# Batch 1's k'q moved from bare steps to pairs beside expert blocks, with the first block one step earlier

## The chip, the core and the metric

The kernel runs on one core of one Trainium2 chip. The time is the device time of one execution in microseconds (us), as the median of several runs. TensorE (PE in the rows) multiplies matrices and has a weight load that runs beside it (PEld). VectorE is DVE, ScalarE is ACT, GpSimd is POOL. SyncE (SP) issues most of the DMAs. POOL issues the indirect ones, which write rows to computed addresses.

## What is computed

Four batches of attention over channels, and then a mixture of experts over all 20224 tokens. In short:

```python
# B, N, C = 4, 5056, 256; 8 experts of 256 -> 1024 -> 256
qn = q / norm(q, axis=1);  kn = k / norm(k, axis=1)
a  = softmax(kn.T @ qn / tau)             # 256 x 256 per batch
x  = v @ a                                # tokens x 256
e  = argmax(x @ w_gate + modality_bias[modality_id])
out[t] = softmax_prob[t, e] * relu(x[t] @ w1[e]) @ w2[e]
```

Everything is in float32. Each product is made of three products of rounded halves (high by high, high by low, low by high).

## The kernel before

A batch is cut into ten steps of 512 tokens (the last has 448), so there are 40 steps in all, numbered g = 0 to 39. The kernel has four kinds of work.

- **k'q** (`kq_pieces(b, s)`, lines 219 to 314) loads 512 rows of q and k, splits each into high and low halves (ACT line 257, DVE line 258), squares them for the norms (ACT line 272, added up by DVE line 274) and multiplies them into the batch's 256 by 256 matrix (PE lines 283 and 287). In the steps named in `SELF`, the norm comes from PE instead (line 294), and the square and the addition fall away. A whole batch of it must be done before that batch's softmax.
- **softmax** (`softmax_pieces`) turns the matrix into the weights of the batch.
- **v a** (`va_pieces(b, s)`) loads 512 rows of v, transposes them (PE line 460), multiplies them by the weights (PE line 476, 24 matmuls of 264 columns), routes each token to its expert (DVE lines 485 to 533, with three small matmuls `rp`, lines 512 to 514), and writes the rows to the expert's list `xs` in memory by four indirect DMAs (POOL line 407).
- **an expert block** (`block_pieces`) takes 512 rows of one expert from `xs` (SP line 596), loads that expert's weights in two halves (SP lines 615 and 619), splits them (lines 634 and 635), transposes the rows (`xtp`, PE line 645), and multiplies twice (`hp`, line 663, and `y`, line 683). There are 40 blocks.

Batch 0's k'q runs alone at the start. Then the loop at line 767 goes through the steps. In step g it interleaves the v a of step g, the k'q of the next batch for the same step number, and a block if one is due. After the step, `pick` (lines 553 to 582, on DVE) chooses an expert that has 512 rows waiting, and if none has, a spare block of padding. `slots_by(g)` says how many blocks are to be chosen after step g: the first after step 3. A block runs `LAG` = 4 steps after its choice, so the first in step 7. Its loads are issued one step ahead, and its first weight split and its transposes (`prep`) stand at the end of the step before it. Blocks that do not fall in the 40 steps run one after another behind them: seven of them.

The text's order is not yet the order of the queues. The framework lays out each engine's queue ahead of time with a planner: it takes the earliest instruction in the text whose inputs and buffer are there by the planner's own estimate of durations, and so pulls later work forward into a gap that it expects. On the chip each queue then runs in that order and waits where the estimate was short.

Buffers limit what can be pulled forward. The q and k tiles of batch 1 have two buffers each, and those of steps 2, 3 and 4 borrow the three buffers of the expert weights (`w1r`, `w2r`). The split halves have two buffers per half step, with the buffers of the blocks (`xh`, `xl`, `hh`, `hl`) lent to the early steps, as the conditions on `START` say.

Of the kernel before, what the change touches and what calls it, by code (L numbers as in the profile page):

```python
# [18 lines left out]

def _interleave(*streams):  # L20

    lists = [list(s) for s in streams if s]
    total = [len(x) for x in lists]
    at = [0] * len(lists)
    while any(a < n for a, n in zip(at, total)):
        i = min(
            (i for i in range(len(lists)) if at[i] < total[i]),
            key=lambda i: ((at[i] + 0.5) / total[i], i),
        )
        lists[i][at[i]]()  # L30
        at[i] += 1
# [3 lines left out]
def kernel(  # L35
# [20 lines left out]
    NS = -(-N // STEP)  # L56
# [14 lines left out]
    LAG = 4  # L71

    SELF = {
        "q": [{1, 4, 7}, set(), set(), set()],
        "k": [set(range(NS)), set(range(4)), set(), set()],
    }
    START = 3

    def parts(s):
        return P if s < NS - 1 else PL  # L80
# [137 lines left out]
    def kq_pieces(b, s):  # L218
        pp = parts(s)
        st = {}  # L220
        t0 = s * STEP

        def load():
            if s == 0:
                gram[b] = [
                    ps1.tile([P, 2 * C], F32, tag=f"{'y' if b == 0 else 'g'}{m}", name=f"g{m}_{b}")
                    for m in range(CH)
                ]
                acc[b] = p1.tile([P, 2, 2 * C], F32, tag="acc", name=f"acc_{b}", bufs=2)
                for n in ("k", "q"):  # L230
                    if SELF[n][b]:
                        selfp[n, b] = ps2.tile([P, CH, 2 * P], F32, tag="h", name=f"self{n}_{b}")
                        norm[n, b] = p1.tile([P, CH], F32, tag=f"n{n}", name=f"n{n}_{b}")
            for n, src, tag in (("q", q, "w1r"), ("k", k, "w2r")):
                if (b == 0 and s % 5 >= 2) or (b == 1 and 2 <= s < START + 2):
                    st[n] = p3.tile([P, TT, C], F32, tag=tag, name=f"{n}_{b}_{s}")
                else:
                    st[n] = p2.tile([P, TT, C], F32, tag=n, name=f"{n}_{b}_{s}")
                rows = src[b, t0 : t0 + pp * TT, :].rearrange("(p t) c -> p t c", t=TT)
                if b == 0 and s == 0:  # L240
                    st[n + "rows"] = rows
                else:
                    nc.sync.dma_start(st[n][:pp], rows)
            if b == 0 and s == 0:
                for h in range(2):
                    ts = slice(2 * h, 2 * h + 2)
                    for n in ("q", "k"):
                        nc.sync.dma_start(st[n][:, ts, :], st[n + "rows"][:, ts, :])

        def split(h):  # L250
            ts = slice(2 * h, 2 * h + 2)
            more = h == 1 and (b == 0 or (b == 1 and s < START + 1))
            qs = p2.tile([P, 2, 2 * C], F32R, tag="xh" if more else "qs", name=f"qs_{b}_{s}_{h}")
            ks = p2.tile([P, 2, 2 * C], F32R, tag="xl" if more else "ks", name=f"ks_{b}_{s}_{h}")
            st[h] = (qs, ks)
            for n, t in (("q", qs), ("k", ks)):
                nc.scalar.copy(t[:pp, :, 0:C], st[n][:pp, ts, :])  # L257
                nc.vector.tensor_tensor(  # L258
                    t[:pp, :, C : 2 * C], st[n][:pp, ts, :], t[:pp, :, 0:C].bitcast(F32), ALU.subtract
                )  # L260
            a = acc[b]
            for n, o in (("q", 0), ("k", C)):
                if s in SELF[n][b]:
                    continue
                first = h == 0 and s == min(set(range(NS)) - SELF[n][b])
                sq = a[:, :, o : o + C]
                if not first:
                    if b == 0 or (b == 1 and s < START + 1):
                        sq = p3.tile([P, 2, C], F32, tag="hh" if n == "q" else "hl", name=f"sq_{b}_{s}_{h}_{n}")
                    else:  # L270
                        sq = p2.tile([P, 2, C], F32, tag="sq", name=f"sq_{b}_{s}_{h}_{n}")
                nc.scalar.activation(sq[:pp], st[n][:pp, ts, :], AF.Square)
                if not first:
                    nc.vector.tensor_tensor(a[:pp, :, o : o + C], a[:pp, :, o : o + C], sq[:pp], ALU.add)  # L274

        def mm(h):
            qs, ks = st[h]
            for t in range(2):
                first = s == 0 and h == 0 and t == 0
                last = s == NS - 1 and h == 1 and t == 1  # L280
                for m in range(CH):
                    g = gram[b][m]
                    nc.tensor.matmul(  # L283
                        g, ks[:pp, t, m * P : (m + 1) * P], qs[:pp, t, :],
                        start=first, stop=False, skip_group_check=True,
                    )
                    nc.tensor.matmul(  # L287
                        g[:, 0:C], ks[:pp, t, C + m * P : C + (m + 1) * P], qs[:pp, t, 0:C],
                        start=False, stop=last, skip_group_check=True,
                    )  # L290
                    for n, x in (("k", ks), ("q", qs)):
                        mine = SELF[n][b]
                        if s in mine:
                            nc.tensor.matmul(  # L294
                                selfp[n, b][:, m, :], x[:pp, t, m * P : (m + 1) * P],
                                x[:pp, t, :].rearrange("p (s c) -> p s c", s=2)[:, :, m * P : (m + 1) * P],
                                start=s == min(mine) and h == 0 and t == 0 and m == 0,
                                stop=s == max(mine) and h == 1 and t == 1,
                                skip_group_check=True,
                            )  # L300
            for n in ("k", "q"):
                if h == 1 and SELF[n][b] and s == max(SELF[n][b]):

                    dg = p1.tile([P, 2 * P], F32, tag="sc", name=f"dg{n}_{b}", bufs=2)
                    for m in range(CH):
                        nc.vector.scalar_tensor_tensor(
                            dg, selfp[n, b][:, m, :], 1.0, ident12, ALU.mult, ALU.mult,
                            accum_out=norm[n, b][:, m : m + 1],
                        )

        yield load
        for h in range(2):
            yield lambda h=h: split(h)
            yield lambda h=h: mm(h)
# [109 lines left out]

    def slots_by(g):

        return max(0, g + 1 - START)

    first_block = LAG + START

# [310 lines left out]
    waiting = []  # L741
# [9 lines left out]
    def block_stream(blk, nxt):  # L751

        once(blk, "load")
        once(blk, "prep")
        body = list(blk["body"])
        if nxt is not None:
            once(nxt, "load")
            done.add((nxt["slot"], "prep"))
            at = [len(body) * (i + 4) // 8 for i in range(len(nxt["prep"]))]
            for o, f in reversed(list(zip(at, nxt["prep"]))):  # L760
                body.insert(o, f)
        before = open_blk[0]["last"] if open_blk[0] is not None else []
        open_blk[0] = blk
        return [blk["first"]] + before + body
# [3 lines left out]
    for g in range(G):  # L768
        b, s = divmod(g, NS)
        streams = []  # L770
        for gg, blk in waiting:
            if gg <= g - LAG + 1:
                once(blk, "load")
        if len(waiting) > 0 and waiting[0][0] <= g - LAG:
            _, blk = waiting.pop(0)
            streams.append(block_stream(blk, waiting[0][1] if waiting and waiting[0][0] <= g - LAG + 1 else None))
        soft = list(softmax_pieces(b)) if s == 0 and b > 0 else []
        streams.append(soft + (va[g + 1][0] if g + 1 < G else []) + va[g][1])
        if b + 1 < B:
            streams.append(list(kq_pieces(b + 1, s)))  # L780
        _interleave(*streams)
        if waiting and waiting[0][0] <= g - LAG + 1:
            once(waiting[0][1], "load")
            once(waiting[0][1], "prep")
        if s == NS // 2 and b + 1 < B:
            setup_bias(b + 1)
        n = slots_by(g)
        while chosen < n:
            waiting.append((g, block_pieces(g, chosen, pick(g, chosen, False), False)))
            chosen += 1  # L790
# [24 lines left out]
    while chosen < NB_MIN or waiting:  # L815
# [5 lines left out]
        _, blk = waiting.pop(0)  # L821
# [62 lines left out]
```

## Time and profile before

| what | value |
|---|---|
| median of 3 runs | 1244.78 us (1243.62 to 1246.61) |
| profiled execution, its own time | 1245.85 us |
| span of the profile | 1243.5 us |
| PE busy | 1221.7 us (98%) |
| DVE busy | 843.9 us (68%) |
| ACT busy | 754.1 us (61%) |
| POOL busy | 348.7 us (28%) |

The span goes from the first instruction to the last. The rows further down are from this one execution, and their times count from its start. Busy times of matmuls overlap, so the time of one in a run of them is read from start to start.

### The profile page before, as it was taken

How to read it: one execution, taken by the hardware profiler on the slowest of the kernel's cores; microseconds unless marked ns; L12 is line 12 of the kernel's file. 1: busy time of each engine (PE TensorE's matmuls, PEld its weight loads, DVE VectorE, ACT ScalarE, POOL GpSimd, SP SyncE). 2: the span in 40 equal slices, each digit the busy share in tenths (PEclk: the TensorE clock that was granted, in tenths of full speed). 3: DMA queues.
4: the chain of work that ended last, by engine and by line, in shares of the span. 5: the costliest groups of instructions: out<-in, count | busy, mean ns of one | idle time of the engine just before them, and what ended most of it. 6: DMA issues, size and time to landing. Idle time of an engine off the chain costs nothing.

```text
span 1243.5 us, 23786 instructions
## 1 busy us (share of the span) xinstructions
PE 1221.7 (98%) x8316; PEld 1116.2 (90%) x8316; DVE 843.9 (68%) x2215; ACT 754.1 (61%) x1531; POOL 348.7 (28%) x348
## 2 busy tenths in 40 slices
PE   8998999999999999999999999999999999999997
PEld 6897899999999999999999999999999999999997
DVE  7898967777777666866776776566655666665552
ACT  7885866666666666766666665565555555545553
POOL 0036343132222222322222222222332222321121
PEclk9998999999999999999999999999999999999999
DMA  9758864555555555555555554444554443467320
GB/s 322 252 191 282 271 205 151 161 190 186 176 170 172 178 171 171 162 176 170 170 181 186 175 167 136 136 134 143 164 173 154 149 153 121 147 211 219 119 95 28
DMA packets 113026, 215.06 MB, mean 173 GB/s; under 512 B 16128, under 2 KB 61696, under 8 KB 112896
## 3 DMA queue, kind: packets, MB, share of 16 engines
q1 hardware_dynamic: 97632, 171.84, 44.3%
q0 software_dynamic: 15264, 41.60, 8.8%
q8 instruction: 67, 1.10, 0.4%
q14 instruction: 63, 0.52, 0.1%
HBM read 167.06 MB, written 46.34 MB: 172 GB/s over the span
## 4 chain that ended last, share of the span: by engine, by line
PE 90%; DVE 3%; issue 3%; DMA 2%; ACT 1%; POOL 1%; SPq 0%; POOLq 0%; DVEq 0%; ACTq 0%
PE y L683 33%; PE hp L663 33%; PE xp L476 9%; PE g L283 5%; PE g L287 3%; PE vtp L460 3%; PE xtp L645 2%; DMA q<-in_q_dram 1%; PE selfk L294 1%; DVE acc L274 1%; POOL out_dram L407 1%; DMA xs<-x,pi 0%; PE ns L329 0%; DVE qs L258 0%; DVE w2l L635 0%
## 5 line engine op out<-in xcount | busy, mean ns | idle before, releaser
L683 PE MATMUL y<-w2h,hh 128*128 128x256 f32 x1264 | 356.7, 282 | 0.0
L407 POOL DMA_INDIRECT xs<-x,pi x160 | 173.0, 1081 | 647.8 <-ACT w1h L634 483.2
L683 PE MATMUL y<-w2l,hh 128*128 128x256 f32 x1264 | 352.7, 279 | 0.0
L683 PE MATMUL y<-w2h,hl 128*128 128x256 f32 x1264 | 351.4, 278 | 0.0
L669 DVE SCALAR_TENSOR_TENSOR hl<-hp,hh 128x512 fp32r<-128x512 f32 (+1 forms) x320 | 216.2, 676 | 147.0 <-ACT hh L668 146.8
L668 ACT ACTIVATE hh<-hp 128x512 fp32r<-128x512 f32 (+1 forms) x320 | 190.1, 594 | 169.2 <-PE hp L663 167.2
L663 PE MATMUL hp<-xh,w1h 128*128 128x512 f32 (+1 forms) x640 | 255.8, 400 | 0.3 <-ACT xh L650 0.3
L663 PE MATMUL hp<-xl,w1h 128*128 128x512 f32 (+1 forms) x640 | 250.3, 391 | 0.0
L663 PE MATMUL hp<-xh,w1l 128*128 128x512 f32 (+1 forms) x640 | 249.7, 390 | 0.0
L683 PEld LDWEIGHTS y<-w2h,hh 128*128 128x128 f32 x1264 | 237.5, 188 | 12.0 <-ACT yo L694 0.2
L683 PEld LDWEIGHTS y<-w2l,hh 128*128 128x128 f32 x1264 | 238.1, 188 | 10.0
L683 PEld LDWEIGHTS y<-w2h,hl 128*128 128x128 f32 x1264 | 236.6, 187 | 0.1
L407 POOL DMA_INDIRECT out_dram<-yo,xr x158 | 163.0, 1032 | 157.5 <-ACT yo L694 113.3
L635 DVE TENSOR_TENSOR w2l<-w2r,w2h 128x512 fp32r<-128x512 f32 x160 | 110.2, 689 | 71.9 <-ACT w2h L634 71.9
L635 DVE TENSOR_TENSOR w1l<-w1r,w1h 128x512 fp32r<-128x512 f32 x160 | 109.8, 686 | 55.5 <-ACT w1h L634 55.1
L634 ACT CAST w2h<-w2r 128x512 fp32r<-128x512 f32 x160 | 100.1, 625 | 74.9 <-PE y L683 67.4
L663 PEld LDWEIGHTS hp<-xh,w1l 128*128 128x128 f32 x640 | 120.1, 188 | 26.2
L634 ACT CAST w1h<-w1r 128x512 fp32r<-128x512 f32 x160 | 101.0, 631 | 60.0 <-PE hp L663 55.7
L663 PEld LDWEIGHTS hp<-xl,w1h 128*128 128x128 f32 x640 | 120.5, 188 | 14.1 <-DVE xl L651 0.4
L663 PEld LDWEIGHTS hp<-xh,w1h 128*128 128x128 f32 x640 | 120.1, 188 | 13.6 <-ACT xh L650 0.5
L283 PE MATMUL g<-qs,ks 128*128 128x512 f32 (+1 forms) x320 | 121.4, 402 | 5.7 <-ACT ks L257 5.7
L476 PE MATMUL xp<-ah,vh 128*128 128x264 f32 x320 | 96.9, 303 | 0.0
(152 smaller groups left out, 1833.0 us busy)
## 6 DMA issues: line engine op xcount, KB each, us to landing
w1r<-in_moe_w_dram SPq DMA_DIRECT2D x80, 512.0 KB, 3.5
w2r<-in_moe_w_dram SPq DMA_DIRECT2D x80, 512.0 KB, 3.7
xr<-xs SPq DMA_DIRECT2D x38, 516.0 KB, 4.7
v<-in_v_dram SPq DMA_DIRECT2D x36, 512.0 KB, 5.3
q<-in_q_dram SPq DMA_DIRECT2D x35, 512.0 KB, 7.5
k<-in_k_dram SPq DMA_DIRECT2D x35, 512.0 KB, 9.8
xs<-pad SPq DMA_DIRECT2D x9, 516.0 KB, 5.6
xs<-x,pi POOLq DMA_INDIRECT x160, 5.1
```

Source lines behind the costliest of these rows:

```text
L283: nc.tensor.matmul(g, ks[:pp, t, m * P : (m + 1) * P], qs[:pp, t, :], start=first, stop=False, skip_group_check=True,)
L287: nc.tensor.matmul(g[:, 0:C], ks[:pp, t, C + m * P : C + (m + 1) * P], qs[:pp, t, 0:C], start=False, stop=last, skip_group_check=True,)
L407: ins = nc.gpsimd.indirect_dma_start(out=dst, out_offset=bass.IndirectOffsetOnAxis(ap=idx, axis=0), in_=rows, in_offset=None, bounds_check ...
L460: nc.tensor.matmul(tp[:, t * P : (t + 1) * P], st["v"][:, t, h * P : (h + 1) * P], ident, is_transpose=True, start=t == 0, stop=True, skip ...
L476: nc.tensor.matmul(xp[:, 0:DE], a[:, h, t * P : (t + 1) * P], w[:, h, :], start=i == 0, stop=i == len(seq) - 1,)
L634: nc.scalar.copy(hi, src)
L635: nc.vector.tensor_tensor(lo, src, hi.bitcast(F32), ALU.subtract)
L645: nc.tensor.matmul(tp[:, t * P : (t + 1) * P], st["xr"][:, t, h * P : (h + 1) * P], identr, is_transpose=True, start=t == 0, stop=True, sk ...
L663: nc.tensor.matmul(hp[:, 0:rows], w[:, h, fs], x[:, h, 0:rows], start=i == 0, stop=i == len(seq) - 1)
L668: nc.scalar.activation(hh[:, 0:rows], hp[:, 0:rows], AF.Relu)
L669: nc.vector.scalar_tensor_tensor(hl[:, 0:rows], hp[:, 0:rows], 0.0, hh[:, 0:rows].bitcast(F32), ALU.max, ALU.subtract)
L683: nc.tensor.matmul(y, a[:, tsl], w[:, j % 2, :], start=(j == 0 and i == 0 and t % 2 == 0), stop=(j == NJ - 1 and i == 2), skip_group_check ...
```

## The change

Five things change together. `START` goes from 3 to 2: the first block is chosen after step 2 and runs in step 6. `SKIP` = 12 leaves out the choice after step 12, and from step 16 on `lag` is 3 instead of 4, so that there is a block in every step from 6 to 39 and six behind them. `PLAN` says which k'q steps of batch 1 stand in which step of batch 0: 0, 1 and 2 in their own, none in 3, 4 and 5, then 3 in step 6, and 4 to 9 in pairs in steps 7, 8 and 9. Batch 1 takes the k norm from PE in steps 0 to 2 only, no longer in 3. And the borrowed buffers go to k'q steps under `AHEAD` = 3 alone. The v a of step 6 also uses the PSUM buffers of later steps, since `first_block` is now 6.

```diff
-        "k": [set(range(NS)), set(range(4)), set(), set()],
+        "k": [set(range(NS)), set(range(3)), set(), set()],
     }
-    START = 3
+    START = 2
+
+    PLAN = [[0], [1], [2], [], [], [], [3], [4, 5], [6, 7], [8, 9]]
+    SKIP = 12
+    AHEAD = 3
...
-                if (b == 0 and s % 5 >= 2) or (b == 1 and 2 <= s < START + 2):
+                if (b == 0 and s % 5 >= 2) or (b == 1 and 2 <= s < AHEAD):
...
-            more = h == 1 and (b == 0 or (b == 1 and s < START + 1))
+            more = h == 1 and (b == 0 or (b == 1 and s < AHEAD))
...
-                    if b == 0 or (b == 1 and s < START + 1):
+                    if b == 0 or (b == 1 and s < AHEAD):
...
-        return max(0, g + 1 - START)
+        return max(0, g + 1 - START - (g >= SKIP))
+
+    def lag(g):
+
+        return LAG if g < SKIP + LAG else LAG - 1
...
-            if gg <= g - LAG + 1:
+            if gg <= g + 1 - lag(g + 1):
                 once(blk, "load")
-        if len(waiting) > 0 and waiting[0][0] <= g - LAG:
+        if len(waiting) > 0 and waiting[0][0] <= g - lag(g):
...
-            streams.append(list(kq_pieces(b + 1, s)))
+            steps = PLAN[s] if b == 0 else [s]
+            streams.append([f for i in steps for f in kq_pieces(b + 1, i)])
         _interleave(*streams)
-        if waiting and waiting[0][0] <= g - LAG + 1:
+        if waiting and waiting[0][0] <= g + 1 - lag(g + 1):
```

## Rows read from the trace of the kernel before

**Rows 1.** The page, part 1: engine, busy us, share of span, instructions.
```profile
PE 1221.7 (98%) x8316; PEld 1116.2 (90%) x8316; DVE 843.9 (68%) x2215; ACT 754.1 (61%) x1531; POOL 348.7 (28%) x348
```

**Rows 2.** Windows, two block steps: length, busy per engine, clock, DMA.
```profile
116.00:146.00 30.00, 29.10 (x191) 25.32 (x192) 28.21 (x76) 20.65 (x44) 7.02 (x8) 1.00 0.93 314
236.00:266.00 30.00, 30.00 (x206) 27.32 (x205) 21.98 (x63) 19.23 (x40) 9.51 (x8) 1.00 0.54 176
```

**Rows 3.** Waits of PE, 50 to 116 us: total, times, longest.
```profile
PE rp L512 <- DVE pki L579: 4.1, 1, 4.1
...
PE rp L513 <- DVE run L507: 0.6, 1, 0.6
PE hp L663 <- ACT xh L650: 0.3, 1, 0.3
PE rp L512 <- DVE oh L499: 0.2, 1, 0.2
```

**Rows 4.** Windows ahead of the first block.
```profile
105.00:110.00 5.00, 2.61 (x12) 2.30 (x13) 4.35 (x24) 4.20 (x9) 3.19 (x4) 0.60 1.02 374
110.00:115.00 5.00, 5.00 (x31) 4.80 (x29) 3.99 (x18) 3.79 (x9) 3.73 (x2) 0.72 0.92 235
```

**Rows 5.** Timeline of PE, one k'q group: start, us, instruction.
```profile
84.50 0.39 PE L283 MATMUL g<-qs,ks 128*128 128x512 f32 x1
...
84.85 0.28 PE L294 MATMUL selfk<-ks 128*128 128x256 f32 x1
84.97 0.40 PE L283 MATMUL g<-qs,ks 128*128 128x512 f32 x1
```

**Rows 6.** Timeline of PE up to block 0; brackets: idle before, releaser.
```profile
107.39 0.21 PE L512 MATMUL rp<-oh,trim 128*128 128x32 bf16 x1 [4.14 <-DVE pki L579]
...
112.45 0.56 PE L283 MATMUL g<-qs,ks 128*128 128x512 f32 x1
...
114.75 0.81 PE L645 MATMUL xtp<-identr,xr 128*128 128x128 f32 x8
115.89 0.73 PE L663 MATMUL hp<-xh,w1h 128*128 128x512 f32 x2 [0.33 <-ACT xh L650]
```

**Rows 7.** Timeline of POOL: scatters 1, 12 and 16.
```profile
79.90 1.19 POOL L407 DMA_INDIRECT xs<-x,pi  x1 [34.73 <-ACT sq_q L272]
...
94.64 1.38 POOL L407 DMA_INDIRECT xs<-x,pi  x1 [0.30 <-issue]
...
103.02 0.97 POOL L407 DMA_INDIRECT xs<-x,pi  x1 [0.30 <-issue]
```

**Rows 8.** Chain of waits, 60 to 150 us: start, us, what.
```profile
73.33 1.47 PE xp L476 x12
...
103.02 5.84 DMA xs<-x,pi
```

**Rows 9.** Timeline of SP: block 0's rows.
```profile
109.29 0.35 SPq L596 DMA_DIRECT2D xr<-xs  x1
```

**Rows 10.** The page, part 6: DMA, count, KB each, median us to landing.
```profile
xr<-xs SPq DMA_DIRECT2D x38, 516.0 KB, 4.7
...
xs<-x,pi POOLq DMA_INDIRECT x160, 5.1
```

**Rows 11.** Timeline of DVE: an addition, addresses of step 0, totals of step 2.
```profile
73.76 0.68 DVE L274 TENSOR_TENSOR acc<-acc,sq_q 128x512 f32<-128x512 f32 x1
...
78.76 0.20 DVE L528 TENSOR_REDUCE pi<-pos 128x4 int32<-128x32 f32 x1
...
83.17 0.16 DVE L519 TENSOR_TENSOR bs<-bs,rp 128x8 f32<-128x8 f32 x1 [0.17 <-PE rp L514]
```

**Rows 12.** Timeline of ACT: block 0's first split, a square of k'q 9.
```profile
104.90 0.62 ACT L634 CAST w1h<-w1r 128x512 fp32r<-128x512 f32 x1 [4.11 <-DMA w1r<-in_moe_w_dram]
...
145.90 0.64 ACT L272 ACTIVATE sq_q<-q 112x512 f32<-112x512 f32 x1 [0.84 <-DMA q<-in_q_dram]
```

**Rows 13.** DMAs on tile xs, 75 to 180 us.
```profile
DMA to landing us min/median/max: 2.8/5.0/7.2
```

More of the change, by code (lines that the diff above doesn't have):

```diff
@@ L20, in _interleave @@
 def _interleave(*streams):
-    lists = [list(s) for s in streams if s]
+    lists = [list(s) for s in streams if len(s) > 0]
     total = [len(x) for x in lists]
@@ L771 @@
         for gg, blk in waiting:
-            if gg <= g - LAG + 1:
+            if gg <= g + 1 - lag(g + 1):
                 once(blk, "load")
-        if len(waiting) > 0 and waiting[0][0] <= g - LAG:
+        if len(waiting) > 0 and waiting[0][0] <= g - lag(g):
             _, blk = waiting.pop(0)
-            streams.append(block_stream(blk, waiting[0][1] if waiting and waiting[0][0] <= g - LAG + 1 else None))
+            streams.append(block_stream(blk, waiting[0][1] if waiting and waiting[0][0] <= g + 1 - lag(g + 1) else None))
         soft = list(softmax_pieces(b)) if s == 0 and b > 0 else []
```

## The prediction

> **What bounds the kernel now.** I read the page's busy shares first, then PE's waits, then the windows and timelines around the first block. PE is busy for 1221.7 of 1243.5 us [rows 1], and a usual step with a block keeps it busy for the full 30.00 us from 236 to 266 us at clock 1.00, with DVE at 21.98 [rows 2]. Every matmul that remains must run on PE, so moving work between steps is worth nothing by itself. The time changes only if matmuls vanish, or if PE loses less, by waiting or by a slow clock. After the softmax of batch 0, those losses stand in one place: the bare steps ahead of the first block. PE waits 4.1 + 0.6 + 0.2 us there on small DVE results, and 0.3 us at the block's first matmul [rows 3]. The 4.1 us begin with ACT, which stands 4.11 us at the block's first weight split until the weights land [rows 12]; DVE, and then PE, run out behind it. After the wait PE's granted clock is 0.60 and 0.72 in two windows [rows 4], and the work from 107.39 to 112.45 us [rows 6] runs at 1.2 instead of 2.4 GHz: 5.06 us for 2.5 us of work, a loss of 2.5 us. Together PE loses 4.9 + 0.3 + 2.5 = 7.7 us there. That is all that an earlier first block can win, and the new order can lose as much again.
>
> **The change part by part.**
>
> *Matmuls removed.* k'q 3 no longer takes the k norm from PE: 8 matmuls (four row groups, two halves of the channels) of 0.12 us (84.85 to 84.97) [rows 5], about 0.9 us. In its place come two squares on ACT and two additions of 0.68 us on DVE [rows 11], off the path in a step where a block keeps PE busy; without that cover they would cost at most 1.4 us.
>
> *What PE has left ahead of block 0.* Before, block 0's transposes start at 114.75 us [rows 6], behind all work of steps 0 to 6. After the change only steps 0 to 5 stand ahead of them in the text. So these leave: k'q 3 with its norm, 8 x 0.47 (84.50 to 84.97) = 3.8; k'q 4, 5 and 6, 8 x 0.35 (84.50 to 84.85) = 2.8 each, 8.4 [rows 5]; the 24 matmuls of v a of step 6, 2 x 1.47 = 2.9 [rows 8]; the eight transposes of step 7's v, taken as the 0.8 us of block 0's eight [rows 6]. That is 15.9 us. Taking out the losses ahead of that point as well (4.9 + 2.5), PE could be at block 0 at 114.75 - 15.9 - 7.4 = 91.4 us.
>
> *When the rows of block 0 are there.* It is chosen after step 2, so its load waits for the first 12 scatters instead of 16. POOL issues them one behind the other: the first starts at 79.90, the twelfth at 94.64 us [rows 7], 14.7 us later, and POOL is the limit, since step 2's totals are made at 83.17 us [rows 11]. The first can come earlier, because additions of k'q 3 and later now rank behind the routing of step 0. Four of 0.68 us stand between 73.76 us and its addresses at 78.76 us [rows 11]. Between 0 and 2.4 us are to be won; I take 1.8, as most of them belong to later steps. Then 78.1 + 14.7 = 92.8; landing 5.1 [rows 10] (5.84 in the chain [rows 8]), 97.9; 0.4 until SP issues the load (108.9 to 109.29) [rows 8, 9]; landing 4.7 [rows 10]: 103.1 us. The ends are 101.8 (2.4 us won, a scatter landing of 4.5 us, between the least and the median of [rows 13]) and 105.9 us (nothing won, 5.84 and 5.0 us).
>
> The Trainium skill (DMA: Bandwidth & Descriptors, on the anatomy of one SWDGE DMA) gives about 2.0 us plus bytes over 436 GB/s, which for a scatter of 128 rows of 1032 bytes is 2.3 us. The row has 5.1, so the measurement decides for the sum; by the page the rows would be there 2.8 us sooner, and the sum would be that of the third rival below.
>
> *What fills the gap.* From 91.4 to 103.1 us PE has 11.7 us to fill. The planner pulls k'q forward: the 112-row square of k'q 9, whose step begins some 30 us later, is at 145.90 us already [rows 12]. The next q and k need only their two buffers, which are free early. DVE needs 8 x 0.68 = 5.4 us per k'q and gets the room that the empty steps leave. I take three k'q steps (8.4 us) and the next transposes (0.8): PE is occupied up to 100.6 us and waits 2.5 us. The ends are nothing (11.7 us of waiting) and everything (no wait). I also take the slow clock again, as the nearest row is the wait of 4.14 us that ended in it [rows 4, 6]: 2.5 us, with 0 as the other end.
>
> *The sum.* First matmul of block 0: 103.1 + 1.1 (114.75 to 115.89) + 2.5 = 106.7 instead of 115.89 us, 9.2 us earlier. Work that was done by then and is now still to do: k'q 6 and v a of step 6, 2.8 + 2.9 = 5.7 us. Net: 3.5 us less, the 0.9 us included.
>
> *Pairs beside blocks.* The cost is taken as zero, because the step from 116 to 146 us already holds more than that: with k'q 7, 8 and part of 9 in it, DVE was busy 28.21 of 30 us and PE still 29.10 [rows 2]. The same again in three steps costs up to 2.7 us; that is the upper end, and 0.9 us back the lower, as that step is lightened.
>
> *The rest.* The missing choice after step 12 and the lag of 3 leave each block's load one step ahead and its rows two steps old when it is issued, where four scatters take some 5 us. One block moves from behind the steps into them, at the same matmuls. SP and POOL issue the same DMAs, the k and q loads only later. Zero, with 1 us either way.
>
> The sum is made in an execution of 1245.85 us (span 1243.5), 1.1 us above the median. Set on the median it gives 1244.8 - 3.5 = 1241.3 us.
>
> **The rivals.**
>
> *The queue runs dry (slower).* If the planner expects block 0's rows sooner than POOL delivers them, it puts the block's transposes behind steps 0 to 5 at once and leaves the k'q for its pairs. PE then stands at an instruction that it can't pass. With no k'q pulled forward the net is -3.5 + 8.4 + 0.8 = +5.7 us, 1250.5; with one and the transposes +2.1, 1246.9. It decides from fewer than about 1.8 k'q steps in the gap. For it: block 0's rows landed only as PE reached them before, though PE had lost 7.4 us, so the plan was too hopeful there by about that. Against it: the pulling forward in [rows 12].
>
> *Half filled (no change).* Two k'q steps fit: -3.5 + 2.8 = -0.7, 1244.1 us.
>
> *The rows are early (faster still).* If the scatters land in 2.8 us [rows 13] instead of 5.1, PE finds the rows at 100.8 us with no wait to speak of and no slow clock: -3.5 - 2.3 - 2.5 = -8.3, 1236.5 us. The Trainium skill's page named above speaks for this. Against it, the chain's own 5.84 us [rows 8].
>
> *A spare block is chosen.* With fewer rows waiting, a choice may find no expert with 512. A count of the reference's routing on its inputs finds one in every choice, at the least 569 rows, after step 11; so it is nearly excluded. It would add a block of 48 x 0.23 + 96 x 0.12 us, 22 us or more.
>
> **How the numbers follow.** Forecast 0.42, its own range 1239 to 1244; dry queue 0.27; half filled 0.19; early rows 0.09; pairs that starve PE or a spare 0.03. What a measurement can tell from no change is 0.2%, 2.5 us. The forecast gives faster 0.36 and the early rows 0.09: 0.45. Half filled gives 0.17 of no change, the edges of the forecast 0.06 and of the dry queue 0.04: 0.27. The rest is slower, 0.28. The range reaches from within the early rows, 1238, to most of the dry queue, 1249.
>
> **What would show it.** Right: the first `hp` at 105 to 108 us, at least two k'q steps of PE ahead of it, one PE wait of 1 to 4 us at `xtp` ending with the load of xr, a clock below 1 behind it, scatters starting at about 78 us, and no PE wait over 1 us in steps 7 to 9. Wrong: a PE wait of 7 us or more ahead of `xtp`; scatters that start no sooner; PE waits on `hh` or `hl` in the paired steps; or PE busy less by something other than the 0.9 us.

## The result, and the profile after

The changed kernel takes 1249.91 us in the median of 8 runs (1248.05 to 1252.38); the kernel before, run beside it, takes 1245.09 us (8 runs, 1243.62 to 1246.61). The ratio is 1.0041, 95% interval [1.0031, 1.0052]: slower, by 5 us. The forecast was 1241.3 us, so it had the wrong sign; its first rival, the queue that runs dry, had 1250.5 us. The profiled execution took 1249.92 us (span 1247.7), against 1245.85 us (span 1243.5) before. One execution of one experiment further down (twice later, 1837.69 us at a granted clock of 0.609) fell in a slower state and is left out; all other times are of fast executions.

The profile's first part, answering to [rows 1]: the busy time of PE is what it was (1221.7), with eight matmuls fewer. No matmul was added, so the time must have gone into waits or into the clock.

```profile
PE 1222.1 (98%) x8308; PEld 1115.1 (89%) x8308; DVE 845.8 (68%) x2217; ACT 759.4 (61%) x1533; POOL 349.2 (28%) x348
```

PE's waits from 50 to 116 us, answering to [rows 3]: total, times, longest. Before, 4.9 us stood on small results of DVE and 0.3 us on the block's first matmul. Now there are 8.5 us in three waits, and a wait for block 0's rows (`xr`) is among them.

```profile
PE rp L520 <- DVE sm L540: 4.0, 1, 4.0
PE xtp L653 <- DMA xr<-xs: 3.5, 1, 3.5
...
PE xp L484 <- ACT x L488: 1.0, 1, 1.0
```

The timeline of PE up to block 0, answering to [rows 6] (start, length, instruction, in brackets the idle time before it and its releaser). After the last k'q matmul (`g`) PE idles at `rp`, then at once at `xtp`. Block 0 starts 9.2 us earlier than before (106.67 instead of 115.89 us), as predicted to the tenth of a microsecond, though by luck, as the part on the prediction shows; and still the kernel is slower.

```profile
95.00 0.39 PE L484 MATMUL xp<-ah,vh 128*128 128x264 f32 x1 [0.99 <-ACT x L488]
...
96.88 0.63 PE L287 MATMUL g<-qs,ks 128*128 128x512 f32 x2
101.53 0.21 PE L520 MATMUL rp<-oh,trim 128*128 128x32 bf16 x1 [4.02 <-DVE sm L540]
105.27 1.10 PE L653 MATMUL xtp<-identr,xr 128*128 128x128 f32 x7 [3.53 <-DMA xr<-xs]
...
106.67 1.22 PE L671 MATMUL hp<-xh,w1h 128*128 128x512 f32 x2
```

The windows ahead of the block, answering to [rows 4] (length; busy time of PE, PEld, DVE, ACT and POOL; PE's granted clock; DMA share; GB/s). PE works 0.21 of 5 us in the second window, and all of its work in the third is at the lower of the clock's two levels (0.50 is 1.2 of 2.4 GHz).

```profile
95.00:100.00 5.00, 2.51 (x14) 1.94 (x14) 4.00 (x17) 3.96 (x10) 4.09 (x4) 1.00 0.85 314
100.00:105.00 5.00, 0.21 (x1) 0.10 (x1) 2.19 (x12) 1.70 (x4) 4.08 (x4) 0.64 0.75 208
105.00:110.00 5.00, 4.70 (x18) 3.83 (x19) 3.10 (x11) 1.17 (x2) 3.78 (x5) 0.50 1.00 356
110.00:115.00 5.00, 5.00 (x28) 4.35 (x27) 3.33 (x11) 2.31 (x4) 3.27 (x4) 0.84 1.04 384
```

What PE did not have there is seen by counting the k'q matmuls of 512 columns (`g`) from 75 to 116 us; a k'q step has eight. The kernel before (count; shortest, median and longest ns; first and last start):

```profile
L283 PE MATMUL g<-qs,ks x31: 387/395/775, 80.6 to 114.4; 128*128 128x512 f32 x31
```

The same line of the changed kernel:

```profile
L287 PE MATMUL g<-qs,ks x10: 388/396/403, 86.4 to 97.1; 128*128 128x512 f32 x10
```

Before, nearly four k'q steps were done there; now one and a quarter. PE's next k'q matmuls come beside the blocks:

```profile
139.28 0.39 PE L291 MATMUL g<-qs,ks 128*128 128x256 f32 x2
```

They belong to k'q 4, as the count of the matmuls from step 0 on shows. ACT had made all high halves of k'q 4 ahead of block 0, the last of them in this row of its timeline, 38 us earlier:

```profile
101.08 0.61 ACT L261 CAST ks<-k 128x512 fp32r<-128x512 f32 x1
```

Of the low halves DVE made one at 92.96 us and the other three from 108.82 to 115.42 us, behind block 0's start but still 24 us ahead of PE.

Block 0's rows are the wait that ends last. The first and the twelfth scatter on POOL's timeline, answering to [rows 7]:

```profile
81.02 1.19 POOL L411 DMA_INDIRECT xs<-x,pi  x1 [8.51 <-ACT vh L472]
...
96.55 1.35 POOL L411 DMA_INDIRECT xs<-x,pi  x1 [0.30 <-issue]
```

The addresses that the first scatter needs, on DVE's timeline, answering to [rows 11]:

```profile
79.89 0.19 DVE L536 TENSOR_REDUCE pi<-pos 128x4 int32<-128x32 f32 x1
```

The load of the rows on SP's timeline, answering to [rows 9]:

```profile
100.93 0.35 SPq L604 DMA_DIRECT2D xr<-xs  x1
```

The addresses are not earlier than before but 1.1 us later (79.89 instead of 78.76). The routing of step 0 begins on DVE at 73.58 instead of 72.26 us, and four additions of the norms (at 75.08, 75.88, 76.64 and 79.28 us) still stand between it and the addresses, as before. The twelve scatters take 15.5 us instead of 14.7. Then it is 4.4 us to the load and 4.3 to the rows at 105.27 us.

The wait of 4.02 us comes from ACT and DVE, which each work in order. ACT, answering to [rows 12]: the weight splits wait for DMAs (0.77, 0.27 us) and the `ex` of the routing stands behind them.

```profile
97.90 0.62 ACT L642 CAST w1h<-w1r 128x512 fp32r<-128x512 f32 x1 [0.77 <-DMA w1r<-in_moe_w_dram]
...
99.92 0.62 ACT L642 CAST w2h<-w2r 128x512 fp32r<-128x512 f32 x1 [0.27 <-DMA w2r<-in_moe_w_dram]
100.44 0.22 ACT L499 ACTIVATE ex<-lm 128x32 f32<-128x32 f32 x1
```

DVE then waits for `ex` and makes the `oh` that PE's `rp` needs:

```profile
100.70 0.19 DVE L539 TENSOR_REDUCE sm<-ex 128x4 f32<-128x32 f32 x1 [0.90 <-ACT ex L499]
...
101.26 0.21 DVE L507 TENSOR_TENSOR oh<-val,vm 128x32 bf16<-128x32 f32 x1
```

Had this wait not been there, PE would have stood at `xtp` from 97.7 us instead. The rows alone set 105.27 us.

A second loss stands later. Windows of three stretches (columns as above): ahead of block 0, its first steps, and the steps in which the changed kernel has its pairs. The kernel before:

```profile
75.00:115.00 40.00, 35.12 (x250) 32.44 (x247) 34.41 (x156) 27.97 (x69) 27.20 (x26) 0.91 0.66 200
115.00:150.00 35.00, 33.77 (x225) 29.55 (x224) 32.69 (x91) 24.59 (x51) 8.60 (x10) 1.00 0.91 306
150.00:250.00 100.00, 99.92 (x687) 91.17 (x686) 74.98 (x198) 68.30 (x140) 34.90 (x33) 1.00 0.56 178
```

The changed kernel:

```profile
75.00:115.00 40.00, 31.36 (x209) 27.55 (x210) 30.83 (x156) 24.22 (x61) 26.16 (x24) 0.87 0.81 266
115.00:150.00 35.00, 35.00 (x244) 32.10 (x244) 28.22 (x70) 22.70 (x45) 9.89 (x10) 1.00 0.64 215
150.00:250.00 100.00, 97.63 (x651) 87.95 (x650) 74.97 (x194) 68.86 (x141) 28.36 (x27) 1.00 0.56 181
```

In the third stretch PE idles for 0.08 us before and 2.37 us after; the largest waits seen in it are 1.3 and 0.7 us of `rp` for DVE's `oh`.

So there is a ledger. Idle time is a window's length less PE's busy time. The loss by the clock is (1 - granted clock) times PE's busy time, over the four windows from 95 to 115 us: for the kernel before 0.40 x 2.61 + 0.28 x 5.00 = 2.4 us [rows 4], for the changed one 0.36 x 0.21 + 0.50 x 4.70 + 0.16 x 5.00 = 3.2 us. PE's busy time is modelled and some records can be missing, so a line of it is good to perhaps half a microsecond. The kernels of the last two groups of experiments are in it as well, against the kernel before's span of 1243.5 us; "work" is the 0.9 us of the removed matmuls, and 5.9 us where an experiment adds some. Sums are made before rounding.

| kernel | idle 75-115 | idle 115-150 | idle 150-250 | slow clock | sum | sum less before, with work | span less before |
|---|---|---|---|---|---|---|---|
| before | 4.9 | 1.2 | 0.1 | 2.4 | 8.6 | | |
| changed | 8.6 | 0.0 | 2.4 | 3.2 | 14.2 | +4.7 | +4.2 |
| own steps | 5.6 | 0.2 | 0.2 | 1.3 | 7.3 | -2.2 | -3.0 |
| late pairs | 7.0 | 1.4 | 2.0 | 2.7 | 13.0 | +3.5 | +3.1 |
| both early | 0.8 | 3.2 | 2.2 | 0.0 | 6.2 | -3.3 | -3.2 |
| twice ahead | 5.2 | 0.4 | 1.8 | 1.3 | 8.7 | +5.1 | +5.2 |
| twice later | 9.1 | 0.0 | 1.3 | 3.1 | 13.5 | +9.8 | +9.5 |
| changed, fourth group | 8.3 | 0.0 | 2.3 | 2.9 | 13.5 | +3.9 | +4.5 |

It closes within 0.8 us in every line. For the changed kernel it says: 3.8 us more idle ahead of block 0, 0.8 more by the clock, 2.3 more beside the pairs, 1.2 less in the block's first steps, 0.9 of work gone. Each line is of one execution. Those of own steps and both early lie 2.9 and 2.5 us under their kernels' medians, the others within 1.3 us; by the medians own steps and both early are equal to the kernel before, not 3 us faster.

### The profile page after: what moved, and what is told of

It reads as the page before. It is cut to its first block, busy times and chain, and to the rows that moved or that the text cites. A ratio compares the mean times of both kernels' runs of the same rounds, so it can differ in the third digit from the quotient of the medians.

```text
span 1247.7 us, 23784 instructions
## 1 busy us (share of the span) xinstructions
PE 1222.1 (98%) x8308; PEld 1115.1 (89%) x8308; DVE 845.8 (68%) x2217; ACT 759.4 (61%) x1533; POOL 349.2 (28%) x348
## 4 chain that ended last, share of the span: by engine, by line
PE 89%; DMA 3%; DVE 3%; issue 3%; ACT 1%; POOL 1%; POOLq 0%; SPq 0%; DVEq 0%; ACTq 0%
PE hp L671 33%; PE y L691 33%; PE xp L484 8%; PE g L287 5%; PE vtp L468 3%; PE g L291 3%; PE xtp L653 2%; DMA q<-in_q_dram 1%; DMA k<-in_k_dram 1%; PE selfk L298 1%; DVE acc L278 1%; POOL out_dram L411 1%; PE ns L333 0%; DMA xr<-xs 0%; DMA xs<-x,pi 0%
```

## The experiments

Theory A: the k'q that was moved behind block 0 is what PE lacks ahead of it; its queue runs dry there and can't pass the block's transposes. Theory B: the pairs beside the blocks cost the time. Theory C: the earlier choice, the missing one after step 12 and the shorter lag cost it. Each ratio is to the kernel before on the same chip. The first three groups, of four runs each, ran on chips on which the kernel before itself takes 1286 to 1294 us; the fourth and fifth ran on chips on which it takes 1244 and 1245 us, and the ledger is made from these and the first measurement. "Bare steps" are those without a block.

**First group.** Own steps: everything as in the changed kernel, but each k'q in its own step.

```diff
-    PLAN = [[0], [1], [2], [], [], [], [3], [4, 5], [6, 7], [8, 9]]
+    PLAN = [[0], [1], [2], [3], [4], [5], [6], [7], [8], [9]]
```

> The changed kernel with every k'q of batch 1 back in its own step; first block in step 6, skipped choice, lag and buffers stay as changed. Theory A (TensorE's queue runs dry: ahead of block 0's transposes it holds only k'q 3 and 2 matmuls of k'q 4): in this queue k'q 3, 4 and 5 all stand ahead of the transposes, 5.5 us more of work, so the waits of 4.0 and 3.5 us shrink by about that and the time falls by 5 to 8 us, to 1241 to 1245. Rival B (the pairs in steps 7 to 9 make VectorE and ScalarE late): the pairs are gone, so it falls as well, but the waits ahead of block 0 stay. Rival C (the earlier choice, the skipped one or the lag cost the time): it stays at 1249 to 1250.

Measured: 1.0019 [0.9994, 1.0044]; no difference from the kernel before. No run of the changed kernel stands beside it on this chip, and the interval is too wide to tell the theories apart.

Late pairs: k'q 3 and 4 back, the pairs left beside the blocks.

```diff
-    PLAN = [[0], [1], [2], [], [], [], [3], [4, 5], [6, 7], [8, 9]]
+    PLAN = [[0], [1], [2], [3], [4], [], [], [5], [6, 7], [8, 9]]
```

> The changed kernel with k'q 3 and 4 in their own steps, none in steps 5 and 6, 5 in step 7, and the pairs 6, 7 and 8, 9 in steps 8 and 9. Theory A: the queue again holds k'q 3 and 4 and half of 5 ahead of block 0, so it gains like the kernel with own steps less 1.4 us, 1242 to 1246. Rival B: two of three pairs stay, so at most a third of the loss goes, 1248 or more.

Measured: 1.0034 [1.0008, 1.0061]; nearer to what theory B expected.

Plan alone: the kernel before with nothing but the new order of k'q; the first block still in step 7.

```diff
+    PLAN = [[0], [1], [2], [], [], [], [3], [4, 5], [6, 7], [8, 9]]
...
-            streams.append(list(kq_pieces(b + 1, s)))
+            steps = PLAN[s] if b == 0 else [s]
+            streams.append([f for i in steps for f in kq_pieces(b + 1, i)])
```

> The kernel before (first block in step 7, lag 4 throughout, the old buffers) with the moved k'q alone. Theory A: its queue ahead of block 0 lacks k'q 3 to 6, 12 us, while the rows still land at about 114 us; losses of 7 us are there already, so it is slower than before by 8 to 14 us, 1253 to 1259, with a TensorE wait of 10 us or more ahead of the transposes. Rival B: as much slower as the changed kernel, about 1250. Rival C: the same as before, 1245.

Measured: 1.0111 [1.0059, 1.0163]. The order of k'q is slower on the old schedule too, so it doesn't need the earlier choice to cost time. Theory A's 8 to 14 us came (12.8), but not its single wait of 10 us: PE's longest from 50 to 125 us is 3.4 us. Theory C has little left.

Known expert: the changed kernel, but block 0 takes the weights of expert 4 without waiting for its choice.

```diff
-                st["e"] = nc.sync.value_load(pki[0:1, 1:2], min_val=0, max_val=E - 1)
+                st["e"] = 4 if slot == 0 else nc.sync.value_load(pki[0:1, 1:2], min_val=0, max_val=E - 1)
```

> The changed kernel, where block 0 loads the weights of expert 4 without waiting for its choice (expert 4 is what it chooses on these inputs). This takes away ScalarE's wait for the weights and with it TensorE's 4.0 us on the routing. Theory A: the rows of block 0 land no sooner, so the 4.0 us move into the wait at its transposes, and the time changes by less than 1.5 us, 1248 to 1250. Rival D (the wait for the weights is a cost of its own): 4 us less, 1246 or under.

Measured: 1.0101 [1.0053, 1.0149], as the changed kernel in the next group. Neither expected time came, and no run of the changed kernel stands beside this one. Its trace has no wait at `xtp`; PE waits 8.7 us for ACT's copies instead. So the run does not decide what the choice of the weights costs.

**Second group.** The changed kernel and own steps again, side by side.

> The changed kernel as it is, as the yardstick for the runs beside it. All theories: slower than the kernel before by 0.3 to 0.5%, ratio 1.003 to 1.005.

> The changed kernel with every k'q of batch 1 in its own step, once more, as the runs of the first time were spread too widely to tell 0.2% apart. Theory A (the queue ahead of block 0 is short by k'q 4 and 5): 5 us or more under the changed kernel, ratio to the kernel before 0.996 to 1.000, no TensorE wait at block 0's transposes. Rival C (the earlier choice, the skip or the lag cost the time): the same as the changed kernel, 1.003 or more.

Measured: the changed kernel 1.0101 [1.0074, 1.0127], own steps 0.9996 [0.9974, 1.0018]. On this chip the order of k'q by itself carries the whole loss. It is more than twice that of the first measurement, 13 us. The changed kernel's PE timeline on this chip shows where the rest is: two waits that the first profile has as one of 0.99 us.

```profile
92.87 0.59 PE L484 MATMUL xp<-ah,vh 128*128 128x264 f32 x1 [5.36 <-ACT x L488]
...
98.56 0.59 PE L484 MATMUL xp<-ah,vh 128*128 128x264 f32 x1 [3.76 <-ACT x L488]
```

ACT stands 3.73 and 5.31 us at its copies in front of them, and the trace does not name what released them ("remote"). What that is stays open. The k'q matmuls that PE still has stand behind these waits in its queue.

Spare rows: block 0 takes its rows from the spare block, which no scatter writes; the block's output rows are left out.

```diff
-            r = nc.sync.value_load(pki[0:1, 0:1], min_val=0, max_val=E * CAP)
+            r = E * CAP if slot == 0 else nc.sync.value_load(pki[0:1, 0:1], min_val=0, max_val=E * CAP)
...
-                after(ins.ins, written[before])
+                if slot > 0:
+                    after(ins.ins, written[before])
+                else:
+                    tc.declare_no_dep(ins.ins, group=f"x{before}", reason="the spare block's rows")
```

> The changed kernel, where block 0 reads its 512 rows from the spare block of padding, which is there from the start, so that its load waits for no scatter; the output rows of that block are left out, all matmuls and DMAs stay. Theory A: the wait of 3.5 us for the rows goes, the one of 4.0 us for the weights stays and with it most of the slow clock: 3 to 6 us under the changed kernel, ratio 0.999 to 1.002. Rival B (the pairs): no change against the changed kernel.

Measured: 1.0053 [1.0033, 1.0074], about half of the loss back, 6.4 us by the medians. The expected ratio, made for the smaller loss of the first measurement, was missed.

Both early: spare rows and known expert together.

> The changed kernel with block 0's rows from the spare block and its weights those of expert 4, loaded without waiting for the choice; the output rows of that block are left out. Theory A: all three waits ahead of block 0 go (1.0 + 4.0 + 3.5 us) and with them the slow clock (2.5 to 5 us): 10 to 13 us under the changed kernel, ratio 0.993 to 0.997. Rival B: no change against the changed kernel; rival D (the weights are a cost of their own): 4 us under.

Measured: 1.0081 [1.0049, 1.0112]. Theory A had expected a gain, and this failed. In the profile block 0's transposes start at 109.16 us, although neither rows nor weights hold them: PE waits for ACT's copies (4.81 and 2.59 us) in the bare steps, and ACT's copy behind the longer wait stands 6.07 us, again "remote". The test was repeated in the last group.

**Third group.** The changed kernel and own steps a third time; own buffers (own steps, with the old number of buffers and the k norm of step 3 on PE again); and one pair placed early.

```diff
-    PLAN = [[0], [1], [2], [], [], [], [3], [4, 5], [6, 7], [8, 9]]
+    PLAN = [[0], [1], [2], [3], [4, 5], [6], [7], [8], [9], []]
```

> The changed kernel once more, beside two with k'q back. If TensorE's queue runs dry ahead of block 0 (theory A): 1.004 to 1.011 of the time before, and between 75 and 115 us TensorE busy at most 32 of 40 us, with most of the idle time ahead of the first hp. If the pairs beside the blocks cost the time (theory B): the same ratio, with the idle time behind 115 us. If the earlier choice costs it (theory C): the same ratio here and in the next run.

> k'q in its own steps, all else as in the changed kernel. Theory A: 0.997 to 1.001 of before (k'q 3, 4 and 5 stand ahead of block 0 again, 8.4 us of filler less the steps' start at full clock), TensorE busy at least 4 us longer in 75 to 115 us than in the changed kernel. Theory B says the same of the time, but with the difference behind 115 us. Theory C: 1.004 or more, as the changed kernel.

> k'q in its own steps and with the old buffers, and selfk of step 3 back: only the choice, step 12 and the lag are new against the kernel before. Theories A and B: 0.997 to 1.003, within 0.2% of own steps (selfk costs 0.9 us of TensorE). Theory C: 1.004 or more. If it is under 0.998 the earlier choice is worth having by itself.

> One pair, but early: k'q 4 and 5 in step 4, 6 in step 5 and so on, one k'q ahead of the kernel before's order and none in step 9. Theory A: as own steps or up to 2 us faster (0.995 to 1.001), since k'q 3 to 5 stand ahead of block 0 and 6 right behind its first matmuls. Theory B (a pair costs what it shares with a step): over own steps by 0.2% or more. A new wait is possible: k'q 5's q and k have to be loaded one step earlier, beside block 0's weights, and then the first xs or the first hp waits for a DMA.

Measured: changed 1.0079 [1.0059, 1.0099]; own steps 0.9987 [0.9965, 1.0008]; own buffers 1.0014 [0.9997, 1.0031]; early pair 0.9998 [0.9975, 1.0021]. Theory C, which expected 1.004 or more, falls: own buffers has the choice, step 12 and the lag of the changed kernel and runs like the kernel before, within its interval. It is 0.27% above own steps, where 0.2% at most was expected; the intervals overlap. A pair as such isn't slow either, if it stands ahead of the first block. PE is busy 27.0 of 40 us from 75 to 115 us in the changed kernel and 33.1 in own steps (14.29 + 12.75 and 18.50 + 14.63), where theory A expected at least 4 us more.

**Fourth group.** Is the time ahead of block 0 empty? The matmuls of v a in steps 4 and 5 are done twice (48 more), and as a control those of steps 13 and 14.

```diff
-            for i, (a, w, h) in enumerate(seq):
-                nc.tensor.matmul(
+            for _ in range(2 if g in (4, 5) else 1):
+                for i, (a, w, h) in enumerate(seq):
+                    nc.tensor.matmul(
...
```

> The changed kernel with TensorE made to do the 24 xp matmuls of each of steps 4 and 5 twice (the same sums once more into the same PSUM tiles): 48 matmuls more, worth 5.9 us at 0.1225 us each (twelve took 1.47 us), all of them queued ahead of block 0. If that stretch is time in which TensorE has nothing to do (theory A), they cost 0 to 2 us: at most 0.2% over the changed kernel beside it, or a gain of up to 2 us where they keep the clock up. If TensorE's own work there sets when block 0 starts (theory D), +5.9 us, 0.45% over the changed kernel.

> The control: the same 48 extra matmuls, but in steps 13 and 14, in the first half of batch 1, where TensorE is busy throughout. Both theories: +5 to +6 us over the changed kernel beside it (0.38 to 0.47%). If it costs nothing either, TensorE has slack there too, and the first run tells nothing.

> The changed kernel beside the two, as their base: 1.004 to 1.011 of the time before.

Measured: the changed kernel 1249.33 us, 1.0036 [1.0024, 1.0048]; twice ahead 1251.33 us, 1.0057 [1.0042, 1.0072]; twice later 1255.9 us (four executions), 1.0095 [1.0079, 1.0112]. The same work costs 2.0 us ahead of block 0 and 6.6 us later, where 5 to 6 were expected. Theory D of this group, that PE's own work there sets the block's start, would have had 5.9 us twice. About two thirds of the extra work cost nothing: it went into empty time, and the loss by the clock fell to 1.3 us. PE's waits with twice ahead, from 60 to 125 us: the wait at `rp` has shrunk from 4.0 to 1.4 us, that at `xtp` for the rows is 3.0 instead of 3.5 us.

```profile
PE xtp L654 <- DMA xr<-xs: 3.0, 1, 3.0
PE rp L521 <- DVE oh L508: 1.4, 1, 1.4
PE xp L485 <- ACT x L489: 0.8, 2, 0.4
```

**Fifth group.** Own steps, late pairs and both early once more, on a chip as fast as the first.

> k'q in its own steps, all else as in the changed kernel, once more. In the changed kernel the 48 extra matmuls cost 2.0 us ahead of block 0 and 7.2 us in steps 13 and 14, so about two thirds of that stretch is empty. Theory A (k'q is what was missing there): 5 to 8 us faster than the changed kernel, 0.996 to 1.000 of before; the waits of TensorE for rp, xp and xtp ahead of block 0 at most 4 us in sum (8 us in the changed kernel). Theory C (the earlier choice costs the time): 1.003 or more.

> k'q 3 and 4 in their own steps, 5 to 9 late, with two pairs beside blocks. Theory A: between own steps and the changed kernel, nearer to own steps (0.998 to 1.002), since 1.5 steps of k'q more stand ahead of block 0 (4.2 us at 2.8 us each). Theory B (the pairs beside the blocks cost the time): 1.003 or more, as the changed kernel.

> The changed kernel with block 0 on the spare block's rows and on expert 4's weights, so that it waits neither for the scatters nor for the choice; that block's output rows are left out. Theory A by the rows (the queue is dry because block 0's rows are late): its transposes start by 98 us and it is 4 to 8 us faster than the changed kernel, 0.997 to 1.001. Theory A by the queue (without k'q TensorE waits anyway, for the xp copies and the routing of steps 3 to 5): at most 3 us faster than the changed kernel, 1.001 or more, and the waits ahead of block 0 stand on xp and rp.

Measured: own steps 1.0006 [0.9994, 1.0017]; late pairs 1.0036 [1.0023, 1.0049]; both early 0.9995 [0.9986, 1.0003].

Own steps has the loss back, by one line of the text and with all else as in the changed kernel. It is 0.7 us above the upper end of what theory A expected, 4 us faster than the changed kernel where 5 to 8 were expected, and its waits ahead of block 0 are 5.0 us where at most 4 were. Its k'q matmuls from 75 to 116 us:

```profile
L287 PE MATMUL g<-qs,ks x23: 387/397/494, 80.9 to 101.7; 128*128 128x512 f32 x23
```

Its windows (the profiled run lies 3 us under the kernel's median):

```profile
75.00:115.00 40.00, 34.41 (x234) 29.31 (x233) 32.51 (x158) 28.01 (x68) 25.59 (x26) 0.96 0.82 269
115.00:150.00 35.00, 34.80 (x236) 31.55 (x235) 34.15 (x83) 27.04 (x56) 12.87 (x9) 1.00 0.83 266
150.00:250.00 100.00, 99.76 (x688) 91.29 (x687) 71.65 (x189) 65.31 (x133) 31.16 (x32) 1.00 0.53 168
```

With 23 `g` instead of 10 ahead of the block, PE idles 5.6 instead of 8.6 us, and from 150 to 250 us 0.2 instead of 2.4. The rows are no earlier, and PE still waits for them on its timeline:

```profile
106.08 0.85 PE L653 MATMUL xtp<-identr,xr 128*128 128x128 f32 x8 [3.84 <-DMA xr<-xs]
```

Late pairs has k'q 3 and 4 ahead of the block and isn't faster than the changed kernel. Theory A's figure (0.998 to 1.002) failed here and theory B's (1.003 or more) came; the place isn't theory B's alone. ACT stood 4.87 us at block 0's first weight split, before it made `vh`; DVE stood behind it at `w1l`, and PE behind DVE. ACT's timeline:

```profile
98.22 0.62 ACT L642 CAST w1h<-w1r 128x512 fp32r<-128x512 f32 x1 [4.87 <-DMA w1r<-in_moe_w_dram]
```

DVE's timeline:

```profile
98.87 0.69 DVE L643 TENSOR_TENSOR w1l<-w1r,w1h 128x512 fp32r<-128x512 f32 x1 [3.65 <-ACT w1h L642]
...
100.20 0.68 DVE L473 TENSOR_TENSOR vl<-vtp,vh 128x512 fp32r<-128x512 f32 x1
```

PE's timeline:

```profile
100.94 0.39 PE L484 MATMUL xp<-ah,vh 128*128 128x264 f32 x1 [4.56 <-DVE vl L473]
```

That is the stall of the kernel before (4.11 us on ACT [rows 12]), back with a wait for `vl` in place of `rp`. PE's k'q matmuls, its filler, were used up before it: the last `g` starts at 95.9 us.

Both early shows theory A by the rows: with rows and weights free, block 0's transposes start at 93.79 us, PE idles 0.8 us from 75 to 115 us, and the clock stays at 1.00. Block 0's transposes on PE's timeline, and the window:

```profile
93.79 0.45 PE L656 MATMUL xtp<-identr,xr 128*128 128x128 f32 x4
...
75.00:115.00 40.00, 39.19 (x286) 35.20 (x284) 35.41 (x166) 25.92 (x63) 25.56 (x24) 1.00 0.80 265
```

The kernel is 0.41% faster than the changed kernel by the fourth group's ratio (0.9995 against 1.0036, 5 us); it leaves out block 0's output rows. But it is no faster than the kernel before. PE idles 3.2 us from 115 to 150 us: its longest wait begins at 114.2 us, where ACT stands at a square of k'q and PE waits for the copy behind it. PE's timeline:

```profile
117.11 0.39 PE L484 MATMUL xp<-ah,vh 128*128 128x264 f32 x1 [2.89 <-ACT x L488]
```

ACT's timeline:

```profile
115.64 0.63 ACT L276 ACTIVATE sq_k<-k 128x512 f32<-128x512 f32 x1 [4.64 <-DMA k<-in_k_dram]
```

In the ledger's third stretch all kernels with the pairs beside the blocks idle 1.3 to 2.4 us (changed 2.37 and 2.30, late pairs 2.00, both early 2.16, twice ahead 1.84, twice later 1.26); the two without them, before and own steps, 0.08 and 0.24. So theory B has its part, about 2 us. Whether the pairing costs it or only that k'q comes later is not shown: no run has one without the other beside the blocks on these chips.

No version beats the kernel before. Own steps is equal to it on every chip, within its intervals.

## Why the prediction was wrong

The failed step is "What fills the gap". It read from a square of k'q 9 on ACT, early by some 30 us [rows 12], that the planner pulls k'q forward, and put three k'q steps (8.4 us) and transposes into PE's gap. ACT's order was no evidence for PE's, and the trace of the kernel before had shown it: PE's first matmul of k'q 9 comes 42 us after that square, in its own step.

```profile
187.59 0.39 PE L283 MATMUL g<-qs,ks 112*128 112x512 f32 x1
```

The changed kernel has ten `g` ahead of block 0, the eight of k'q 3 and two of k'q 4, 8 x 0.35 + 2 x 0.23 = 3.3 us instead of 9.2, and no transposes of step 7's v. Twice ahead shows that the gap was empty, own steps that k'q fills part of it.

Point by point, against the forecast of -3.5 us:

- *Matmuls removed*, 0.9 us: eight fewer on the page. Right in number.
- *PE could be at block 0 at 91.4 us*: PE's last matmul ahead of the two waits ended at 97.5 us; less 3.3 us of k'q and 1.0 us of waiting that is 93.2 us. That is 1.8 us late and makes the gap shorter: -1.8.
- *The rows at 103.1 us*: 105.27, inside the ends given (101.8 to 105.9). The 1.8 us that the first scatter was to win became a loss of 1.1, and the train of twelve was 0.8 us longer; both landings were quicker than the 5.1 and 4.7 us that were taken. The additions that were to fall back stayed. +2.2. The rival of the early rows did not come: the twelfth scatter's DMA takes 4.13 us in the chain of waits of this trace, and the median landing from 80 to 101 us is 4.4. The trace does not agree with the estimate of 2.3 us, worked out for a scatter from the fit in the Trainium skill (DMA: Bandwidth & Descriptors, Anatomy of one DMA — SWDGE (gpsimd) path).
- *What fills the gap*: 3.3 us instead of 9.2. +5.9.
- *The slow clock*, 2.5 us: 3.2. +0.7.
- *Pairs beside blocks*, 0 us with 2.7 as the upper end: 2.3. The step from 116 to 146 us was a fair row for the size of the loss (29.10 of 30 us busy) but not for none.
- *The rest*, 0 us: 1.2 us less idle from 115 to 150 us. Own buffers, with the choice, the skip and the lag alone, shows no cost clear of its interval (up to 0.3%). -1.2.

The sum is -3.5 - 1.8 + 2.2 + 5.9 + 0.7 + 2.3 - 1.2 = +4.6 us; the span grew by 4.2, the median by 4.8.

The rival of the dry queue had the sign, the place and the mechanism: PE stands at an instruction that it can't pass. Its 5.7 us came near the measured 4.8 partly by chance: it supposed no k'q at all in the gap and no cost of the pairs, where 3.3 us were in the gap and the pairs cost 2.3. Its reason, that the planner expects the rows too early, is not shown, since no run shows the planner's estimates; the runs show the order that came of it.

The start of block 0 at 106.7 us came true by two errors that cancel: the rows were 2.2 us late, and from them to the first `hp` it took 1.4 us instead of 1.1 + 2.5, as most of the slow clock fell behind that `hp`. So the credit of 9.2 us for the earlier start was right. What it was set against was not: the work still to do by then was 5.7 us in the sum and, with the k'q that was not done, 5.7 + 5.9 - 1.8 = 9.8 us. An earlier start is worth only what PE has done by then. Own steps starts block 0 at 107.26 us, 8.6 us earlier than before, with the same 6 us of idle time, and its median is that of the kernel before.

What stays open: what holds ACT's copies on the slower chips; why the routing of step 0 began 1.3 us later with less k'q in front; why the planner left the rest of k'q 4 behind the block on PE, with its high halves made; and which of the pair's instructions delays `oh` beside the blocks.

## What to carry to other kernels

Where one engine is busy for 98% of the span, don't count only how much earlier a stage starts: sum the engine's idle time and its slow-clock loss, stretch by stretch, since these and removed work are all that can be won. Work moved out of a stretch that waits for data was that stretch's filler; before it is moved, read on the waiting engine itself, in its program order, what will stand between the last ready instruction and the wait. Early work of the same stage on another engine is no evidence for it: here ACT was 42 us ahead of PE with k'q 9 before, and 38 us with k'q 4 after. Two engines that work in order pass a DMA's delay on: a weight split that waits on ACT stopped DVE's small operations and then PE, in three of the kernels here (before, changed, late pairs).

## What the runs showed of the hardware

PE's granted clock was 0.64 from 100 to 105 us, in a wait of 8 us with 0.2 us of work in it, and 0.50 in the first 5 us of work behind it (105 to 110 us; 0.84 in the next window); with both early PE didn't stop there and the clock was 1.00 from 75 to 150 us. A wait ahead of a block thus costs again after it has ended, here about 3.2 us on 8.6 of idle time.

The same program, the kernel before, took 1244 to 1245 us on the chips of the first measurement and of the last two groups, and 1286 to 1294 us on those of the first three groups, and a change that costs 0.4% on the first costs 0.8 to 1.0% on the second: the changed kernel's pauses ahead of block 0 are longer there (5.36 and 3.76 us at `xp` in the second group). What makes these chips slower is not shown.
